# An attention's score products cut into quarters of TensorE's array

## The chip, the cores and the metric

The kernel runs on one core of a Trainium2 chip. The metric is the device time of one execution in microseconds (us); smaller is better. A core has five engines that run side by side: TensorE (PE in the profile, its weight loads PEld), VectorE (DVE), ScalarE (ACT), GpSimd (POOL) and SyncE (SP, which here only issues DMAs).

## The reference

Two parts follow each other. The first is a causal attention with decay, over 4 batches, 8 heads, 768 positions and a head width of 64; q, k and v are float32:

```
Dmask = where(i >= j, lam[h] ** (i - j), 0)
intra = (qb @ kb.T * Dmask) @ vb            # inside a block of positions
inter = (qb * lam ** (pos + 1)) @ kv_state  # from the blocks before
out   = intra + inter
kv_state = lam ** block * kv_state + (kb * lam ** (block - 1 - pos)).T @ vb
```

The second is a mixer on x, the attention's output as 4 x 768 x 512:

```
u = x + (relu(x.T @ w_tok1) @ w_tok2).T
y = u + relu(u @ w_ch1) @ w_ch2
```

## The kernel before, in words

The kernel takes blocks of 128 positions where the reference takes 64, which is the same sum: 6 blocks for each head. Heads go in pairs: 4 pairs in each of 4 batches make NI = 16 rounds of a loop (line 671). For a pair, kT and qT (made by the transposes of L230, L245 and L238) hold the 64 rows of the head width on 128 partitions: the lower 64 partitions belong to one half of the blocks, the upper 64 to the other half (x = 0 and 1), and along a row stand 6 blocks of 128 positions, three (m) for each head (h).

The function `scores` (line 313) is what the change touches. For each head h, each m and each half x it forms one block of scores, keys by queries: the weights are 64 rows by 128 columns of kT, the moving operand is 64 rows by 128 columns of qT, and the product fills 128 partitions by 128 columns of a PSUM bank sc[x]. That is 12 products for a pair of heads. The two halves x lie on different rows of the array and write different banks. All operands are float32, and the profile shows such a product as two passes, each with a weight load and a matmul, both under one line.

TensorE's order is the program's order; nothing reorders the code. One round i of the loop puts on TensorE, in this order:

- `scores(i + 1)` (L320), 24 passes in the profile;
- `carry(i)` (L348): the contribution of the earlier blocks' state, 10 products of 64x64 weights (tiles sv and st) by 128 columns, each on one quarter of the array (64 rows by 64 columns), 20 passes;
- `outputs(i, 0)` (L361): 6 products of 128x64 weights by 128 columns, 12 passes;
- `state(i + 1)` (L281): 10 products of 128x64 weights (tile kd) by 64 columns, 20 passes on the two column halves of the array;
- `outputs(i, 1)` (L361), 12 passes;
- transposes for round i + 2 (L230, in the first eight pairs L245 too), transposes of the attention's result (L386), and from round 4 on groups of the mixer's first part, `token_hidden` and `token_out` (L499, L520).

In round i = -1 there is no carry and no outputs, and `scores(0)` is followed by `state(0)`; in round 15 there are no scores. So 16 calls of `scores` run, 15 of them straight ahead of a `carry`.

Around them: VectorE multiplies the scores by the mask (`weigh`, L332, four products of 128x384 for a pair); GpSimd makes the scaled queries (L268) and places the states (L302); ScalarE copies results out of PSUM (L233, L368). SyncE issues the loads of q, k and v some rounds ahead. Where an instruction has to wait for more than it can hold itself, a semaphore instruction stands ahead of it in the same program order (EVENT_SEMAPHORE on PEldq in the profile: TensorE's sequencer, which feeds weight loads and matmuls in one stream).

The attention and its transposes end at about 172 us; the rest of the span is the channel part of the mixer (L858, L1059, L1114), with weights that are brought and split while TensorE works.

Of the kernel before, what the change touches and what calls it, by code (L numbers as in the profile page):

```python
# [25 lines left out]
def kernel(  # L26
# [23 lines left out]
    nc = tc.nc  # L50
    B, H, S, D = q.shape
# [3 lines left out]
    P = 128  # L55
# [55 lines left out]
    def bank(tag, nm, n):  # L111
        nonlocal shared
        if tag == "sh":
            tag = f"sh{shared % 3}"
            shared += 1
        return ps.tile([P, n], F32, tag=tag, bufs=4 if tag == "sc" else 1, name=nm)
# [84 lines left out]
    def rows_of(x):  # L201
        return slice(x * D, (x + 1) * D)
# [6 lines left out]
    while n < P:  # L209
        nc.vector.tensor_mul(  # L210
            out=lams[:, :, n : 2 * n], in0=lams[:, :, 0:n], in1=lams[:, :, n - 1 : n].broadcast_to([P, 2 * NP, n])
# [3 lines left out]
    for h in range(2):  # L215
        r = rows_of(h)
# [5 lines left out]
    kTs, qTs, qss, kds, weights_of, scored = {}, {}, {}, {}, {}, {}  # L222
# [90 lines left out]
    def scores(i):  # L313
        for h in range(2):
            scored[i, h] = sc = [bank("sc", f"sc{i}{x}{h}", 3 * P) for x in range(2)]
            for m in range(3):
                ms = slice((3 * h + m) * P, (3 * h + m + 1) * P)
                for x in range(2):
                    r = rows_of(x)
                    nc.tensor.matmul(  # L320
                        out=sc[x][:, m * P : (m + 1) * P],
                        lhsT=kTs[i][r, ms],
                        rhs=qTs[i][r, ms],
                        start=True,
                        stop=True,
                    )

    def weigh(i, h):
        b, p = pairs[i]
# [341 lines left out]
    for i in range(-2, NI):  # L671
# [5 lines left out]
        if 0 <= i + 1 < NI:  # L677
            scores(i + 1)
            scale_q(i + 1)
            weigh(i + 1, 0)  # L680
# [47 lines left out]
        if i in loads:  # L728
            x = loads.index(i)
# [11 lines left out]
        if i in turns:  # L741
            x = turns.index(i)
# [600 lines left out]
    for n in range(NQD):  # L1343
        r, g = divmod(n, NG)
        for s in range(7):
# [69 lines left out]
            else:  # L1415
                if n == NG and s == 0:
                    tasks.extend(lambda q_=q_: mm2(NG - 1, 1 - q_ // 4, q_ % 4) for q_ in range(8))
                if n == NG and s == 1:
                    for i in range(4):
                        x = tp.tile([P, 2, CB], F32R, tag="tt", bufs=4, name=f"tt{i}")  # L1420
                        tiles.extend((x[:, 0], x[:, 1]))
                if n == NG + 1 and s == 1:
                    for i in range(3):
                        for t in ("hh0", "hl0", "hh1", "hl1"):
                            at = dict(tag=t, name=f"{t}x{i}")
# [4 lines left out]
                    for t in ("c2h", "c2l"):  # L1430
                        x = w2b.tile([P, JG, DM], F32R, tag=t, name=f"{t}x")
# [31 lines left out]
        if n == NG - 1:  # L1463
# [8 lines left out]
            for t in ("c2h", "c2l"):  # L1472
                x = wa.tile([P, JG, DM], F32R, tag=t, name=f"{t}x")
# [45 lines left out]
```

## Time and profile before

| what | value |
|---|---|
| time, median of 3 runs | 554.69 us (554.27 to 555.03) |
| span of the profiled execution, first to last instruction | 552.4 us |
| time of the profiled execution around its span | not given; the median stands 2.29 us above the span |
| TensorE matmuls | 537.1 us busy, 97% of the span, 3710 |
| TensorE weight loads | 455.1 us busy, 82%, 3710 |
| VectorE | 386.8 us busy, 70%, 588 |
| GpSimd | 275.9 us busy, 50%, 264 |
| ScalarE | 250.2 us busy, 45%, 463 |
| DMA | 108.12 MB, mean 196 GB/s |

The span counts from the first to the last instruction on the core. Busy time is the time in which at least one instruction of the engine was running. Matmuls overlap, so the time of one group of matmuls is better read from where the groups start than from the length of one. A shape such as 64*128 64x128 means weights of 64 rows and 128 columns and a moving operand of 64 rows and 128 columns. In the timeline, consecutive instructions of one kind are merged to one row: start, time to the end of the last one, engine, line, operation, tiles, shapes, count.

### The profile page before, as it was taken

The numbers are of one execution on the slowest core, as the hardware profiler recorded it, in microseconds if no ns is written. First come the engines' busy times: TensorE is split into PE (matmuls) and PEld (weight loads), VectorE is DVE, ScalarE is ACT, GpSimd is POOL, SyncE is SP. The second block draws the span as 40 slices with busy tenths as digits, with TensorE's granted clock in tenths as the row PEclk, the third lists the DMA queues.
The fourth block names the chain that finished last, engine by engine and source line by source line (L and its number), as shares of the span: only waits on it lengthen the run. The fifth ranks groups of instructions, "written<-read, shape, count | busy, mean of one in ns | idle before, by whom it ended". The sixth has DMA issues, their size and how long they took to land.

```text
span 552.4 us, 9745 instructions
## 1 busy us (share of the span) xinstructions
PE 537.1 (97%) x3710; PEld 455.1 (82%) x3710; DVE 386.8 (70%) x588; ACT 250.2 (45%) x463; POOL 275.9 (50%) x264
## 2 busy tenths in 40 slices
PE   6999999999999999999999999999998999999996
PEld 5888989999999988788888888888886888888885
DVE  4667776677865868688995657498578864474464
ACT  3477544654534456455554344344464343233111
POOL 5555636552442777556769635545878123141000
PEclk9999999999999999999999999999999999999999
DMA  9999878698500497956777899677346987554007
GB/s 188 245 264 220 189 143 222 143 201 199 133 1 6 172 296 253 361 190 250 285 284 268 179 239 304 206 246 273 133 125 211 205 197 294 225 169 156 0 2 151
DMA packets 162942, 108.12 MB, mean 196 GB/s; under 512 B 132560, under 2 KB 147408, under 8 KB 162896
## 3 DMA queue, kind: packets, MB, share of 16 engines
q1 hardware_dynamic: 153168, 86.92, 58.4%
q10 hardware_dynamic: 9728, 20.58, 10.0%
q8 instruction: 29, 0.48, 0.4%
q14 instruction: 17, 0.14, 0.1%
HBM read 75.50 MB, written 31.98 MB: 195 GB/s over the span
## 4 chain that ended last, share of the span: by engine, by line
PE 81%; DVE 6%; ACT 5%; DMA 4%; POOL 2%; issue 2%; SPq 1%; DVEq 0%; ACTq 0%
PE b L858 15%; PE gb L1114 9%; PE po L1059 9%; PE d L858 7%; PE gc L1114 7%; PE ph L499 6%; PE pu L520 5%; PE sc L320 4%; PE xT L361 4%; PE a L858 4%; DMA raw<-in_moe_w_ch_dram 3%; PE xT L348 2%; PE gb L1059 2%; PE gc L1059 2%; PE kv L281 2%
## 5 line engine op out<-in xcount | busy, mean ns | idle before, releaser
L302 POOL COPY st<-sv 64x192 f32<-64x192 f32 (+1 forms) x32 | 15.7, 492 | 58.8 <-DVE sv L289 57.9
L1072 DVE TENSOR_TENSOR uT<-po,uT 128x512 f32<-128x512 f32 x48 | 32.8, 684 | 10.2 <-PE po L1059 9.6
L1059 PE MATMUL po<-hh,c2l 128*128 128x512 f32 x96 | 37.8, 394 | 0.0
L1059 PE MATMUL po<-hl,c2h 128*128 128x512 f32 x96 | 37.7, 392 | 0.0
L1059 PE MATMUL po<-hh,c2h 128*128 128x512 f32 x96 | 37.6, 392 | 0.0
L368 ACT COPY uT<-xT 128x384 f32<-128x384 f32 x32 | 15.2, 479 | 47.2 <-PE xT L361 47.2
L332 DVE TENSOR_TENSOR a<-sc,mask 128x384 f32<-128x384 f32 x64 | 32.1, 543 | 2.4 <-PE sc L320 2.3
L268 POOL TENSOR_TENSOR qs<-qT,lamp 128x384 f32<-128x384 f32 x32 | 32.6, 1040 | 0.0
L879 POOL TENSOR_TENSOR hl1x<-t,hh1x 128x512 fp32r<-128x512 f32 x8 | 10.6, 1326 | 41.8 <-ACT hh1x L873 41.8
L1129 DVE TENSOR_TENSOR uT<-gb,uT 128x512 f32<-128x512 f32 x40 | 26.1, 683 | 3.8 <-PE gb L1114 3.8
L393 DVE TENSOR_TENSOR xlo<-xp,xhi 128x384 fp32r<-128x384 f32 x32 | 17.7, 552 | 15.7 <-ACT xhi L392 15.2
L499 PE MATMUL ph<-xhi,w1h 128*128 128x256 f32 x96 | 28.3, 295 | 0.3 <-DVE hl L504 0.3
L499 PE MATMUL ph<-xhi,w1l 128*128 128x256 f32 x96 | 27.2, 283 | 0.0
L499 PE MATMUL ph<-xlo,w1h 128*128 128x256 f32 x96 | 27.1, 283 | 0.0
L361 PE MATMUL xT<-a,vn 128*64 128x128 f32 x384 | 27.1, 277 | 0.0
L320 PE MATMUL sc<-qT,kT 64*128 64x128 f32 x384 | 27.1, 290 | 0.0
L320 PEld LDWEIGHTS sc<-qT,kT 64*128 64x128 f32 x384 | 23.9, 197 | 3.0 <-issue 1.2
L858 PE MATMUL b<-o,c1h 128*128 128x512 f32 x72 | 25.2, 391 | 0.0
L858 PE MATMUL a<-o,c1h 128*128 128x512 f32 x72 | 25.2, 391 | 0.0
L879 POOL TENSOR_TENSOR tt<-t,tt 128x512 fp32r<-128x512 f32 x12 | 17.0, 1420 | 14.6 <-ACT tt L873 14.6
L520 PE MATMUL pu<-w2h,hh 128*128 128x384 f32 x64 | 23.2, 363 | 0.9 <-DVE uT L525 0.5
L289 DVE TENSOR_TENSOR_SCAN sv<-keep,kv 128x320 f32<-128x320 f32 x16 | 13.1, 816 | 13.3 <-PE kv L281 6.6
(417 smaller groups left out, 1737.6 us busy)
## 6 DMA issues: line engine op xcount, KB each, us to landing
c1h<-k SPq DMA_DIRECT2D x12, 896.0 KB, 5.5
c1l<-k SPq DMA_DIRECT2D x12, 896.0 KB, 7.6
raw<-in_moe_w_ch_dram SPq DMA_DIRECT2D x7, 1024.0 KB, 5.7
vn<-in_v_dram SPq DMA_DIRECT2D x16, 384.0 KB, 6.1
k<-c1h ACTq DMA_DIRECT2D x6, 896.0 KB, 5.2
k<-c1l ACTq DMA_DIRECT2D x6, 896.0 KB, 4.1
out_dram<-y SPq DMA_DIRECT2D x72, 64.0 KB, 2.5
c2lx<-k SPq DMA_DIRECT2D x7, 512.0 KB, 4.2
```

The costliest lines, as they stand in the source:

```text
L268: nc.gpsimd.tensor_mul(out=qss[i][:, h], in0=qTs[i].rearrange("p (h m i) -> p h m i", h=2, i=P)[:, h], in1=lamp[:, p, h, None, :].broadcas ...
L320: nc.tensor.matmul(out=sc[x][:, m * P : (m + 1) * P], lhsT=kTs[i][r, ms], rhs=qTs[i][r, ms], start=True, stop=True,)
L332: nc.vector.tensor_mul(out=a, in0=scored[i, h][x].rearrange("p (c i) -> p c i", i=P), in1=mask[:, 2 * p + h, None, :].broadcast_to([P, 3, P]),
L361: nc.tensor.matmul(out=xT[h * D : (h + 1) * D, m * P : (m + 1) * P], lhsT=vns[i][:, h, c, :], rhs=weights_of[i, x, h][:, m, :], start=Fals ...
L499: nc.tensor.matmul(out=ph, lhsT=w[:, c, fs], rhs=x[:, c], start=(i == 0), stop=(i == 3 * NC - 1))
L520: nc.tensor.matmul(out=pu, lhsT=h[:, kk, cs], rhs=w[:, kk, ss], start=(i == 0), stop=(i == 3 * NK - 1))
L858: nc.tensor.matmul(out=c[into], lhsT=w[:, WI[o], ct], rhs=x[:, ct], start=(first and i == 0), stop=(i == 5), skip_group_check=True,)
L879: nc.gpsimd.tensor_sub(out=B_[key][1], in0=src, in1=B_[key][0].bitcast(F32))
L1059: nc.tensor.matmul(out=po, lhsT=w[:, jj, cs], rhs=h, start=(i == 0), stop=(i == 3 * JG - 1), skip_group_check=n >= NG)
L1072: nc.vector.tensor_add(out=ub, in0=two(po), in1=ub)
L1114: nc.tensor.matmul(out=G[into, t], lhsT=w2[:, v, j, t * P : (t + 1) * P], rhs=x, start=(o in (5, 1, 2) and not second and i == 0), stop=(i ...
L1129: nc.vector.tensor_add(out=ub, in0=two(G[into, t]), in1=ub)
```

## The change

`scores` alone is changed. Each product of 64x128 weights by 128 columns is cut into four: two halves y of the weights' columns (keys) by two halves z of the moving columns (queries). Each small product has 64x64 weights and 64 moving columns, and writes 64 partitions by 64 columns of the same bank: the half y decides the partitions, z the columns. The half x still decides the rows of the array, so that (x, y) names one of four quarters. The order is z outermost, then y, then x. For a pair of heads 48 products stand in the place of 12. What is computed, the banks, the other engines' instructions, the DMAs and the order of everything else are the same.

```diff
             for m in range(3):
-                ms = slice((3 * h + m) * P, (3 * h + m + 1) * P)
-                for x in range(2):
-                    r = rows_of(x)
-                    nc.tensor.matmul(
-                        out=sc[x][:, m * P : (m + 1) * P],
-                        lhsT=kTs[i][r, ms],
-                        rhs=qTs[i][r, ms],
-                        start=True,
-                        stop=True,
-                    )
+                at = (3 * h + m) * P
+                for z in range(2):
+                    for y in range(2):
+                        for x in range(2):
+                            r = rows_of(x)
+                            nc.tensor.matmul(
+                                out=sc[x][rows_of(y), m * P + z * D : m * P + (z + 1) * D],
+                                lhsT=kTs[i][r, at + y * D : at + (y + 1) * D],
+                                rhs=qTs[i][r, at + z * D : at + (z + 1) * D],
+                                start=True,
+                                stop=True,
+                            )
```

## Rows read from the trace of the kernel before

**Rows 1.** The page: busy times, strips of 40 slices, the chain's shares by engine.

```profile
PE 537.1 (97%) x3710; PEld 455.1 (82%) x3710; DVE 386.8 (70%) x588; ACT 250.2 (45%) x463; POOL 275.9 (50%) x264
...
PE   6999999999999999999999999999998999999996
...
PEclk9999999999999999999999999999999999999999
...
PE 81%; DVE 6%; ACT 5%; DMA 4%; POOL 2%; issue 2%; SPq 1%; DVEq 0%; ACTq 0%
```

**Rows 2.** Waits of TensorE, 0 to 175 us: total, times, longest.

```profile
PE kt L230 <- DMA kn<-in_k_dram: 4.3, 1, 4.3
PE qt L245 <- ACT kT L233: 1.8, 6, 0.4
PE pu L520 <- DVE uT L525: 0.5, 1, 0.5
```

**Rows 3.** Chain of waits in order of time, one round: start, us, what, count.

```profile
123.50 1.05 PE pu L520 x6
124.56 1.54 PE sc L320 x24
126.09 0.91 PE xT L348 x19
127.00 0.81 PE xT L361 x12
127.81 0.58 PE kv L281 x20
```

**Rows 4.** Timeline of TensorE's matmuls in the same round.

```profile
124.48 1.61 PE L320 MATMUL sc<-qT,kT 64*128 64x128 f32 x24
126.02 0.38 PE L348 MATMUL xT<-qs,sv 64*64 64x128 f32 x1
126.03 0.33 PE L348 MATMUL xT<-qs,st 64*64 64x128 f32 x2
126.04 0.38 PE L348 MATMUL xT<-qs,sv 64*64 64x128 f32 x1
126.19 0.28 PE L348 MATMUL xT<-qs,st 64*64 64x128 f32 x2
126.24 0.30 PE L348 MATMUL xT<-qs,sv 64*64 64x128 f32 x2
126.30 0.28 PE L348 MATMUL xT<-qs,st 64*64 64x128 f32 x2
...
126.72 0.28 PE L348 MATMUL xT<-qs,sv 64*64 64x128 f32 x1
126.93 0.88 PE L361 MATMUL xT<-a,vn 128*64 128x128 f32 x12
127.63 0.75 PE L281 MATMUL kv<-vn,kd 128*64 128x64 f32 x20
128.21 0.83 PE L361 MATMUL xT<-a,vn 128*64 128x128 f32 x12
```

**Rows 5.** Line 320 in the whole span: duration ns min/median/max, first and last start.

```profile
L320 PEld LDWEIGHTS sc<-qT,kT x384: 182/188/336, 7.8 to 157.5; 64*128 64x128 f32 x192
L320 PE MATMUL sc<-qT,kT x384: 271/272/577, 7.8 to 157.6; 64*128 64x128 f32 x192
```

**Rows 6.** Lines 281 and 230, 36.9 to 38.9 us: the sequencer's semaphore instructions.

```profile
L281 PEldq EVENT_SEMAPHORE  x1: 1272/1272/1272, 37.0 to 37.0; - x1
...
L230 PEldq EVENT_SEMAPHORE  x1: 51/51/51, 38.8 to 38.8; - x1
```

**Rows 7.** Timeline of weight loads, 37.3 to 38.9 us.

```profile
37.57 0.64 PEld L361 LDWEIGHTS xT<-a,vn 128*64 128x64 f32 x12
38.26 0.69 PEld L281 LDWEIGHTS kv<-vn,kd 128*64 128x64 f32 x20
```

**Rows 8.** The page's DMA queues: packets, MB, share of 16 engines.

```profile
q8 instruction: 29, 0.48, 0.4%
```

**Rows 9.** Chain of waits, 185 to 245 us.

```profile
191.05 1.06 PE pu L520 x6
...
192.12 7.91 DMA raw<-in_moe_w_ch_dram
...
232.19 0.62 DVE e L898
```

## The prediction

> **What bounds the kernel now.** I read the page first, then TensorE's waits, the chain of waits, and the timeline of one round. TensorE is busy for 97% of the span, its strip shows nines almost everywhere, and 81% of the chain that ended last is its own [rows 1]. Its waits up to 175 us, the stretch in which all scores lie, come to some 7 us, of which 4.3 are the first load of k [rows 2]. So a microsecond that `scores` gains or loses on TensorE is one on the path, as long as nothing else is late behind it. In the chain the scores of one round are one piece of 1.54 us, followed at once by `carry`, `outputs` and `state` [rows 3]; 16 such pieces are 24.6 us, 4.5% of the span.
>
> [...]
>
> **The scores before, step by step.** 24 passes start between 124.48 and 124.48 + 1.61 - 0.27 = 125.82 us (0.27 is the median length of one) [rows 4, 5]. The row halves run side by side, so these are 12 rounds of two. The first pass waits for its weights: `carry`'s first on sv shows 0.38 us where a later one has 0.28, and I take the same 0.10 for the scores' first, whose weights have twice the columns [rows 4]. So 1.34 - 0.10 = 1.24 us over 11 steps, 0.112 us a round, and the stage's array time is 0.10 + 12 x 0.112 = 1.45 us. From the last start to `carry`'s first start are 126.02 - 125.82 = 0.20 us; 0.11 of it is the last round, the other 0.09 is the array running empty between two kinds of tiles. (`carry` to `outputs` has such a gap too, 126.72 to 126.93; `outputs` to `state`, both on 128x64 tiles, has none [rows 4].) Then `carry`'s first pass spends 0.10 on weights.
>
> **The scores after.** Each product is cut in four, so 96 passes of 64x64 weights by 64 columns take the place of 24. The trace shows no such pass; two rows bracket it. `state` has 64 moving columns and 64 weight columns on two column halves: 20 passes from 127.63 to 128.21, 10 rounds of 0.058 us [rows 4]. `carry` shows four quarters at work at once: four first passes start within 0.02 us, and from there each quarter starts one pass about every 0.11 us (the st pairs at 126.19 and 126.30) with twice the columns of the new pass [rows 4]. Each row of the array would be fed by the new stage just as `state` feeds it, two halves of 64 columns at a time. So I take `state`'s 0.058 us for a round of four: 96 / 4 = 24 rounds, 1.39 us, plus 0.05 for the first weights (half the columns, half the 0.10). The sum is 1.44 us against 1.45: four times the passes gain nothing in the stage itself. If a round cost half of `carry`'s 0.11 for half the columns, 0.055, it would be 0.07 us less a stage, 1.1 us in all; and if a round of four pays more than `state`'s, up to the price of `carry`'s rounds, 0.11, it is 24 x 0.11 = 2.64 us, 1.2 us more. I take 0.058, since it is nearest in columns, weights and traffic a row.
>
> The gain is behind the stage. Scores and `carry` are now the same kind of tile, 64x64. The 0.09 of running empty goes, and `carry`'s first weights load under the scores' last round (0.058 of the 0.10 hidden). That is 0.09 + 0.06 = 0.15 us for each of the 15 calls that are followed by `carry`; `scores(0)` is followed by `state`, on other tiles, and keeps its gap. Ahead of the scores stand 128x128 products as before, so that gap stays.
>
> **Can the sequencer feed it?** One round of 0.058 us takes four weight loads and four matmuls, 0.0145 us for a pair. No stretch of the trace sustains that: `state` runs at 0.029 a pass and `carry` at 0.70 / 20 = 0.035. But both are paced by the array. The sequencer alone shows at 37.0: it is held for 1.27 us ahead of `state`, the first weights load at 38.26, and at 38.8 it is already at the transposes' semaphore, having handed over 20 passes of `state` and 12 of `outputs` meanwhile [rows 6, 7]: 0.54 us for 32 pairs, 0.017 a pair at most (0.49 to 0.59 by the rounding of 38.8). At 0.017 a round is 0.068 and the stage 1.68, unless TensorE's queue is full when the stage begins; in the gap ahead of a stage it has time to fill. Its depth can be seen at 37.0 us: the sequencer is done with all 12 passes of `outputs`, whose first weights load at 37.57, while the last of `carry` are still to run [rows 6, 7], so some 16 pairs wait. 80 x 0.017 = 1.36 is under the 1.39 of the rounds. I take no loss, and 0.24 a stage as the dear end.
>
> Added beside this: 72 passes x 2 x 16 = 2304 instructions. The 7420 that stand there came in 29 packets of code [rows 1, 8], 256 each, so nine more come, each taking 0.4% x 16 x 552.4 / 29 = 1.2 us on the queues. TensorE has no wait that answers to the 29; I cost the nine at nothing, and at 9 x 1.2 = 10.8 us if none is hidden. VectorE gets the first head's scores when half the rounds are over, as before; DMAs and other engines' work do not change.
>
> **The sum.** 15 x 0.15 = 2.25 us off, 16 x 0.01 off for the stage itself, which I leave out. What is late next: behind the attention the chain leaves TensorE once, from a load of raw weights at 192.12 to VectorE at 232.8, where TensorE waits about 0.6 us; but that load follows TensorE's pu at 191.05 to 192.11, so it comes earlier along with it [rows 9]. The span goes from 552.4 to 550.2, and the 2.3 us by which the median stands above the span stay: 552.5.
>
> [...] Side by side, first starts on different quarters stand 0.01 us apart [rows 4]. [...]
>
> **The rivals.**
> - *One pass at a time, or two quarters at a time* (slower). If starts of passes are paced by what the trace has sustained at best, `state`'s 0.029, or if a product's second pass holds back the next quarter so that only two quarters ever work, a stage is 96 x 0.029 = 2.78 us: 1.33 more, less 0.15: 15 x 1.18 + 1.33 = 19 us, 573.7. It decides from the point where a pass costs over (1.45 + 0.15) / 96 = 0.0167 us. For it: nothing below 0.028 is sustained anywhere. Against: the four quarters of `carry`, and the 0.017 of the sequencer.
> - *Rounds a little dearer* (no change). At the sequencer's 0.068 a round the stage is 1.68, 0.23 dearer, and 15 x 0.08 + 0.23 = 1.4 us more: 556.1; at 0.064 the stage is 1.59 and the gain is just used up: 554.7. For it: the queue's depth is only inferred, and four streams write PSUM at once. Against: `carry`'s rounds on four quarters, 0.11, are no longer than those of `outputs` on two halves (126.93 to 127.63, six rounds of 128 columns, 0.117 with the first weights) [rows 4].
> - *Code arrives late* (slower). Nine packets at 1.2 us, less 2.25: 563.2 with none hidden, 557 with half. For it: the new instructions lie within 150 us, in bursts. Against: 29 packets without a visible wait.
>
> **Chances.** Forecast 0.58, its own range 551.4 (rounds of 0.055) to 553.6 (half the gain lost); rounds a little dearer 0.17, half of it within 0.2%, a quarter on either side; one or two at a time 0.15; late code 0.10. The measurement can tell about 0.2%, 1.1 us, from no change. Faster by more: 0.58 + 0.04 = 0.62. Within: 0.08 + 0.04 from late code that costs about what is gained: 0.12. Slower: 0.26. The range reaches from 551.3 up to 561, which leaves out the one-at-a-time rival and the dear half of late code.
>
> **What would show it.** Right: L320 x1536, a stage from first score to first `carry` of about 1.45 us, `carry` starting some 0.06 after the last score pass, without the 0.20; four score passes within 0.06. Wrong: a score stage of over 1.6 us in the chain; passes 0.025 or more apart throughout; new idle time named issue ahead of L320 or L348 where code packets land; or TensorE idle behind 192 us by what was gained ahead of it.

## The result, and the profile after

The kernel with 48 products a pair of heads takes 557.68 us (median, 556.18 to 559.54) against 554.86 us before: ratio 1.0057, 95% interval 1.0041 to 1.0073. It is 2.8 us slower where 2.2 us less was forecast (554.69 to 552.5). The profiled execution took 556.63 us, with a span of 554.8 us against 552.4.

The page after (busy times, instructions; strips; the queue that brings code):

```profile
span 554.8 us, 12049 instructions
...
PE 537.3 (97%) x4862; PEld 456.2 (82%) x4862; DVE 385.8 (70%) x588; ACT 250.3 (45%) x463; POOL 276.8 (50%) x264
...
PE   6899999999999999999999999999999999999996
...
PEclk9989999999999999999999999999999999999999
...
q8 instruction: 38, 0.62, 0.5%
```

Against [rows 1, 8]: 1152 passes more on TensorE and the same busy time; nine more packets of code; and one slice of the clock strip, the third, that was a 9 and is an 8.

The timeline of TensorE's matmuls in the round that answers to [rows 4] (start, us to the end of the last, count at the end):

```profile
127.03 1.63 PE L322 MATMUL sc<-qT,kT 64*64 64x64 f32 x96
128.48 0.32 PE L350 MATMUL xT<-qs,sv 64*64 64x128 f32 x1
128.48 0.28 PE L350 MATMUL xT<-qs,st 64*64 64x128 f32 x2
128.50 0.33 PE L350 MATMUL xT<-qs,sv 64*64 64x128 f32 x1
...
129.13 0.28 PE L350 MATMUL xT<-qs,sv 64*64 64x128 f32 x1
129.33 0.43 PE L363 MATMUL xT<-a,vn 128*64 128x128 f32 x3
```

The part of the prediction that was worked out came as forecast. From the first score to the last are 1.63 - 0.22 = 1.41 us (0.22 is one pass), 0.07 more than the 1.34 of before; `carry` starts 0.04 us behind the last score, where it was 0.20; and from the first score to `outputs` are 129.33 - 127.03 = 2.30 us against 126.93 - 124.48 = 2.45. That is 0.15 us gained, to the hundredth the forecast for a round; the rounds differ by 0.02 around 0.14.

The loss lies elsewhere. TensorE's waits up to 175 us, in the order of [rows 2] (total, times, longest):

```profile
PE kt L230 <- DMA kn<-in_k_dram: 4.7, 1, 4.7
PE xT L363 <- issue: 2.2, 3, 1.9
PE qt L245 <- ACT kT L233: 1.4, 5, 0.3
```

The middle row is new: `outputs` waits for nothing that the profile shows. The chain of waits from 22 us on, and the row of before that answers to its last one:

```profile
22.42 0.74 PE xT L350 x19
23.16 0.81 PE xT L363 x12
23.97 0.58 PE kv L281 x20
24.55 0.44 PE xT L363 x8
24.99 1.89 issue
26.88 0.44 PE xT L363 x4
27.32 1.32 PE kt L230 x6
28.64 1.47 PE qt L245 x6
30.11 1.09 PE xp L388 x6
31.20 1.56 PE sc L322 x96
```

```profile
28.10 1.54 PE sc L320 x24
```

In the middle of `outputs`, after 8 of its 12 passes, TensorE stands still for 1.89 us. The passes behind the standstill read no tile that the passes ahead of it had not read already, so there was no new operand to wait for. What follows is slow: six transposes of k take 1.32 us here and 0.81 in later rounds of the same kernel. The scores that began at 28.10 us begin at 31.20. The stretches of this time (us; busy and count of PE, PEld, DVE, ACT and POOL; granted clock; DMA share; GB/s) say why the transposes are slow:

```profile
24.70:26.90 2.20, 0.31 (x8) 0.17 (x5) 2.20 (x5) 0.00 (x0) 0.93 (x2) 1.00 1.19 255
26.90:28.50 1.60, 1.60 (x11) 1.43 (x11) 0.30 (x1) 0.89 (x2) 0.72 (x1) 0.67 0.96 273
28.50:31.20 2.70, 2.70 (x17) 2.20 (x18) 0.00 (x0) 2.08 (x6) 1.27 (x2) 0.56 1.23 228
31.20:33.00 1.80, 1.80 (x112) 1.80 (x114) 0.30 (x1) 1.80 (x4) 0.69 (x1) 1.00 0.88 276
```

Behind the standstill the granted clock is 0.67 and then 0.56 of full (0.50 from 27.60 to 30.90 us), until the scores of the next pair, where it is 1.00 again. The transposes of k, of q and of the result take 1.32 + 1.47 + 1.09 = 3.88 us; in later rounds, at a granted clock of 1.00, they take 0.81, 1.09 (twice 0.55 for three) and 0.66: 2.56. So the standstill costs 1.3 us more after it has ended.

**What TensorE waited for is its own code.** Counted in the order of their starts, weight loads, matmuls and semaphore instructions together, 962 instructions of TensorE's queue had started when it stood still. Up to 175 us it stood still four more times with no wait to explain it, for 0.3 to 0.4 us each, and always a multiple of 256 instructions from that count:

| instructions started | standstill ended at | last packet of code landed at | between |
|---|---|---|---|
| 962 = 194 + 3 x 256 | 26.88 us | 25.30 us | 1.58 us |
| 1474 = 194 + 5 x 256 | 39.14 | 37.74 | 1.41 |
| 1986 = 194 + 7 x 256 | 49.17 | 47.68 | 1.49 |
| 5314 = 194 + 20 x 256 | 139.41 | 138.20 | 1.22 |
| 5826 = 194 + 22 x 256 | 152.23 | 150.85 | 1.38 |

One packet of q8 is 16 KB (0.62 MB in 38 packets), and I count 256 instructions to it: the five counts lie 512, 512, 3328 and 512 apart, all multiples of 256, and 7514 instructions in 29 packets before and 9818 in 38 after are 259 and 258 to a packet. The number of packets is that of the bounds 194 + 256k that a program crosses: 29 for 7514 instructions before, 38 for 9818 after. In the trace after, up to 175 us, 22 of 25 packets began to move 0.5 to 4.0 us after TensorE had crossed a bound (the other three 0.25 to 1.3 us ahead of it), each moved for 0.9 to 1.4 us, and where TensorE waited for one, it went on 1.2 to 1.6 us after that. No trace shows what calls for a packet; my assumption is that it is called for at one bound and needed at the next: from the bound before to the end of the standstill are 5.6, 6.4, 3.4, 4.2 and 4.1 us in the five rows. Before, the first bounds are crossed at 15.2, 23.3, 31.3 and 39.2 us, 8 us apart, and from the second on the packet has landed over 4 us ahead. After, they are crossed at 10.4, 14.9, 21.2 and (without the standstill) about 24.8 us: 256 instructions in 3.6 us, and the packet is not there. A short block alone does not make a standstill: the one from 82.2 to 85.2 us lasted 3.0 us and passed without one, since its packet had landed at 83.13.

The kernel before crosses 29 bounds, and the waits of its matmuls show no idle time named issue over the whole span. Here TensorE stood still at five of 38 bounds, for 1.89 us at one of them.

The sum: 15 x 0.14 = 2.1 us gained; 3.4 us lost at the five bounds (starts 2.16 us apart where 0.11 is usual, and 0.28, 0.35, 0.40 and 0.33 over the usual); 1.3 us lost to the clock. That makes 2.6 us slower; TensorE's last transpose of the attention starts 2.83 us later than before (172.04 against 169.21 us), and the span is 2.4 us longer. The 1.3 us of the clock belong to this profiled execution: another of the four had a mean granted clock of 1.000 and took 558.73 us, and what it paid instead is open.

### The profile page after: what moved, and what is told of

It is laid out like the page before. It is cut to its first block, busy times and chain, and to the rows that moved or that the text cites. A ratio compares the mean times of both kernels' runs of the same rounds, so it can differ in the third digit from the quotient of the medians.

```text
span 554.8 us, 12049 instructions
## 1 busy us (share of the span) xinstructions
PE 537.3 (97%) x4862; PEld 456.2 (82%) x4862; DVE 385.8 (70%) x588; ACT 250.3 (45%) x463; POOL 276.8 (50%) x264
## 4 chain that ended last, share of the span: by engine, by line
PE 78%; DVE 6%; ACT 5%; DMA 4%; issue 2%; SPq 2%; POOL 2%; DVEq 0%; ACTq 0%
PE b L860 15%; PE gb L1116 9%; PE po L1061 8%; PE d L860 7%; PE gc L1116 7%; PE ph L501 5%; PE pu L522 4%; PE a L860 4%; PE xT L363 4%; PE sc L322 3%; DMA raw<-in_moe_w_ch_dram 3%; PE gb L1061 2%; PE xT L350 2%; PE gc L1061 2%; DMA qn<-in_q_dram 1%
## 5 line engine op out<-in xcount | busy, mean ns | idle before, releaser
L1074 DVE TENSOR_TENSOR uT<-po,uT 128x512 f32<-128x512 f32 x48 | 32.8, 684 | 10.4 <-PE po L1061 9.8
L370 ACT COPY uT<-xT 128x384 f32<-128x384 f32 x32 | 15.2, 480 | 49.3 <-PE xT L363 49.3
L395 DVE TENSOR_TENSOR xlo<-xp,xhi 128x384 fp32r<-128x384 f32 x32 | 17.7, 552 | 18.3 <-ACT xhi L394 17.9
L322 PEld LDWEIGHTS sc<-qT,kT 64*64 64x64 f32 x1536 | 25.0, 139 | 3.5 <-issue 1.3
L322 PE MATMUL sc<-qT,kT 64*64 64x64 f32 x1536 | 27.3, 225 | 0.3 <-ACT qT L246 0.2
L363 PEld LDWEIGHTS xT<-a,vn 128*64 128x64 f32 x384 | 20.6, 137 | 4.4 <-issue 2.4
```

The lines of the kernel that those rows point to most:

```text
L322: nc.tensor.matmul(out=sc[x][rows_of(y), m * P + z * D : m * P + (z + 1) * D], lhsT=kTs[i][r, at + y * D : at + (y + 1) * D], rhs=qTs[i][r ...
L363: nc.tensor.matmul(out=xT[h * D : (h + 1) * D, m * P : (m + 1) * P], lhsT=vns[i][:, h, c, :], rhs=weights_of[i, x, h][:, m, :], start=Fals ...
L1074: nc.vector.tensor_add(out=ub, in0=two(po), in1=ub)
```

## The experiments

Three theories were put against each other: the code theory above; that work on four quarters costs the time itself; that TensorE, being early, meets some wait at that place. The kernel before, run beside the first four, took 554.59 us.

**The same quarters with half the passes.** The columns of the weights are cut (y), the moving columns are not (z):

```diff
-                for z in range(2):
-                    for y in range(2):
-                        for x in range(2):
+                for y in range(2):
+                    for x in range(2):
...
-                                out=sc[x][rows_of(y), m * P + z * D : m * P + (z + 1) * D],
+                            out=sc[x][rows_of(y), m * P : (m + 1) * P],
...
-                                rhs=qTs[i][r, at + z * D : at + (z + 1) * D],
+                            rhs=qTs[i][r, at : at + P],
```

> Scores as 24 products of 64x64 weights by 128 columns, on the same quarters: 48 passes a pair of heads instead of 96 (before: 24). Code theory (TensorE's instructions come in blocks of 256, a block is asked for when the one before is entered, and the changed kernel runs through a block faster than the next one comes): the 0.14 us a round gained between scores and carry stays, as carry is still the same kind of tile, and 768 more instructions than before instead of 2304 leave at most one short stall: 552.3 to 553.5 us, ratio to before 0.996 to 0.998, no idle time named issue over 0.5 us ahead of outputs. Quarters theory (work on four quarters at once costs the time itself): the quarters are as busy as in the changed kernel, so it is slower than before as that one is, 556 to 558. Wait theory (TensorE, being early, meets a semaphore or data wait at the second outputs of round 1): as early as the changed kernel, so the same stall of about 2 us there, 556 to 558.

Measured: 553.12 us, ratio 0.9973, interval 0.9962 to 0.9983. It is faster than both. Its chain of waits in the round of [rows 3]:

```profile
124.65 1.47 PE sc L321 x48
126.12 0.68 PE xT L349 x19
126.80 0.81 PE xT L362 x12
```

Scores and `carry` together take 2.15 us here, 2.45 before, and 1.56 + 0.75 = 2.31 with 48 products. The quarters are used as much as in the slow kernel, at half the instructions, and 32 packets of code come without one standstill by issue of 0.3 us or more in its waits up to 175 us. That rules the quarters theory out, and the wait theory too, since TensorE is earlier still at that place (24.21 us against 24.38 at the start of the second `outputs` of round 1). But 15 x 0.30 = 4.5 us were to be had in this way and 1.5 arrived. Two places keep the rest in the profiled execution. In the first rounds the chain is a load:

```profile
19.15 15.12 DMA qn<-in_q_dram x2
34.27 0.14 issue
34.41 0.30 PE qt L245
```

TensorE waits 2.1 us for q there (two waits), and the seventh call of `scores` starts 1.15 us later than before (55.91 against 54.77 us). The two loads landed at 26.70 and 34.27 us; in the kernel before they landed at 25.32 and 31.84 us, 0.7 and 1.4 us ahead of the transposes that use them, so a gain on TensorE larger than these margins would have met the loads there too, unless they came earlier with it. The DMA strip of the kernel before shows nines in these slices of 13.8 us:

```profile
DMA  9999878698500497956777899677346987554007
```

Why the loads landed later here, no run tells. From the seventh call to the sixteenth it gains 1.86 us in nine rounds, 0.2 each. And where the attention's last transpose is 0.98 us earlier than before, the matmuls behind 230 us are only 0.50 us earlier: in between lie the raw weights' load and conversion of [rows 9]; that these hold it back was not tested.

**Quarters in the late rounds only, and in the early ones only.**

```diff
+                if i < 5:        # the other kernel: if i >= 5
+                    ms = slice((3 * h + m) * P, (3 * h + m + 1) * P)
+                    for x in range(2):
+                        ...      # the 12 old products
+                    continue
```

> The 48 small products only for pairs 5 to 15, the 12 old ones for pairs 0 to 4. Code theory: the long stall of 1.9 us lies in round 1 and is gone, with the slow clock behind it; 11 rounds gain 0.14 each, 1.5 us, and up to three stalls of 0.3 us are given back: 553.3 to 554.4, ratio 0.997 to 0.999. Quarters theory: 11 of 16 parts of the loss of 2.8 us: 556.8. Wait theory: about as the code theory.

> The 48 small products only for pairs 0 to 4, the 12 old ones from pair 5 on. Code theory: the stall of about 2 us in round 1 and the slow clock behind it (1.3 us) are still there, four gains of 0.14 us: 557 to 558, as slow as the changed kernel or slower. Quarters theory: 5 of 16 parts of 2.8 us: 555.7. Wait theory: 557 to 558 too.

Measured: late only 554.29 us, ratio 0.9997 (0.9985 to 1.0009); early only 557.14 us, ratio 1.0040 (1.0028 to 1.0052). Five calls in the early rounds lose nearly as much as all sixteen, and eleven in the late ones lose nothing. The early one's timeline of TensorE has the standstill again, 2.67 us long, after the same 962 instructions and the same 8 passes:

```profile
24.33 0.61 PE L375 MATMUL xT<-a,vn 128*64 128x128 f32 x8
27.61 0.44 PE L375 MATMUL xT<-a,vn 128*64 128x128 f32 x4 [2.67 <-issue]
```

Here the clock did not fall, though the standstill is the longest of all; the stretch behind it reads:

```profile
27.60:29.00 1.40, 1.39 (x13) 1.16 (x12) 0.00 (x0) 0.86 (x3) 0.21 (x1) 1.00 1.13 240
```

Hardly anything else in this kernel gains or loses up to the attention's end: its fourth call of `scores` starts 2.63 us later than before (30.66 against 28.03 us), its last transpose of the attention 2.48 us later (171.69 against 169.21). So a single late block makes up nearly the whole of its 2.55 us.

The late one shows no standstill by issue in its list of waits up to 175 us, and its late rounds gain what they should: its seventh call starts 0.61 us later than before and its sixteenth 0.46 us earlier, 0.12 a round. Yet this does not show in the time. In the profiled execution TensorE waits 0.9 us for a load of q in the early rounds, where the scores are the old ones, and 0.8 us for a copy (snap, ACT) near 390 us. I take the first for the scatter of loads in the rounds that DMA fills, which no run shows; the second is open.

**The bounds moved.** Only the very first call has its old products, so that 144 instructions fewer stand ahead of everything else:

```diff
+                if i == 0:
+                    ...          # the 12 old products
+                    continue
```

> As the changed kernel, but the first call of scores, pair 0, has its 12 old products: 144 instructions fewer ahead of all the rest. Code theory: the bounds of the blocks of 256 fall 144 instructions later in the program. The stall ahead of the 9th pass of the second outputs in round 1 (instruction 962 by count) is gone from there; if any comes, it comes again at instruction 962, now within the scores of pair 3, and shorter, since transposes that wait for copies lie in that block: 0 to 1 us. The short stalls of later rounds move to other lines as well. Time 553 to 556. Quarters theory: within 0.3 us of the changed kernel. Wait theory: the stall stays at the second outputs of round 1, at another count (818), and the time is within 0.3 us of the changed kernel.

Measured: 558.03 us, ratio 1.0053 (1.0040 to 1.0066): no better than the changed kernel, where 553 to 556 was expected. The time alone would fit the quarters theory. The place does not:

```profile
17.36 0.39 PE L375 MATMUL xT<-a,vn 128*64 128x128 f32 x4
19.71 0.55 PE L375 MATMUL xT<-a,vn 128*64 128x128 f32 x6 [1.95 <-issue]
```

The long standstill is gone from round 1 and stands a round earlier, after 450 = 194 + 256 instructions; its packet landed at 18.19 us, 1.5 us ahead of the end. Two more, of 0.31 and 0.72 us, stand at 1474 and 2754, again bounds (194 + 5 x 256, 194 + 10 x 256). So the standstills go by the count, which the wait theory excludes. My expectation erred in looking at the one bound that I knew: a shift lays every bound on another stretch, and the dense stretch of the round before got one. Behind this standstill the clock is low as well: granted 0.68 from 19.7 to 22.3 us and 0.50 from there to 24.0.

**The other half of the cut.** Moving columns cut, weights whole, on the two row halves of before:

```diff
-                ms = slice((3 * h + m) * P, (3 * h + m + 1) * P)
-                for x in range(2):
+                at = (3 * h + m) * P
+                for z in range(2):
+                    for x in range(2):
...
+                            lhsT=kTs[i][r, at : at + P],
+                            rhs=qTs[i][r, at + z * D : at + (z + 1) * D],
```

> The other half of the cut alone: 64x128 weights, 64 moving columns, two row halves, 24 products and 48 passes a pair of heads. As many instructions as the kernel with 64x64 weights by 128 columns, so the code theory sees no stall. The loads of 128 weight columns were 0.107 us apart on a half before, and a pass of 64 columns streams in about 0.055, so the loads set the pace: 24 rounds of 0.107 instead of 12 of 0.112, 1.2 us more a stage, and the gap to carry stays 0.2: 16 x 1.2 = 19 us slower, 573 to 575. If weight loads were hidden or halved with the columns, it would be as before, 554.6.

Measured: 577.79 us against 554.61 beside it, ratio 1.0423 (1.0380 to 1.0465), somewhat above what was expected. The timeline of its scores, and line 321 from 100 to 180 us (min/median/max ns):

```profile
140.57 2.90 PE L321 MATMUL sc<-qT,kT 64*128 64x64 f32 x48
143.40 0.38 PE L349 MATMUL xT<-qs,sv 64*64 64x128 f32 x1
```

```profile
L321 PEld LDWEIGHTS sc<-qT,kT x336: 182/188/188, 103.4 to 178.7; 64*128 64x128 f32 x168
```

48 passes on two halves are 24 rounds, and from first to last start 2.90 - 0.27 = 2.63 us: 0.11 a round, as with 128 moving columns [rows 4]. Halving the moving columns alone shortened nothing; with the weights' columns halved too, on four quarters, a round took 0.06 (24 in 1.41 us). That fits the expectation that the loads of 128 weight columns set the pace. The stage grew by 1.29 us, 16 times 20.6, and the profiled execution (575.33 us) is 20.7 above the median of the kernel before; two of the four runs lie near 580 us, and what those paid is open.

**Code alone, by no-ops.** The old scores, with empty instructions behind each product:

```diff
                         stop=True,
                     )
+                    for _ in range(12):   # the other kernel: 4
+                        nc.tensor.nop("pad")
```

> The kernel before, its 12 products of 64x128 by 128 kept, with 12 empty instructions (no-ops) on TensorE's queue behind each product: 2304 more instructions, as many as the change adds, and no more array work. Code theory: the array's work is as before, but the blocks of 256 are used up as fast as in the changed kernel, so idle time named issue of 1 us or more appears in the first rounds, at counts 256 apart with the no-ops included, and the time is 556 to 560 us. Quarters theory (the quarters cost it): no quarters here, 554.6, unless the no-ops themselves hold up the sequencer, which would show as idle time within the scores of every round. Wait theory (TensorE too early at one place): TensorE is not early, 554.6.

> As the run with 12 no-ops, but with 4 behind each product: 768 more instructions, as many as the kernel with 24 products of 64x64 by 128 adds. Code theory: as that kernel, which showed no stall by code, none here either; no gain between scores and carry, so 554.3 to 555.2, the same as before. If no-ops were dear by themselves, a third of the loss of the run with 12.

Measured: 713.79 us and 572.28 us, ratios 1.2871 (1.2854 to 1.2889) and 1.0326 (1.0301 to 1.0352). Both missed, and neither bears on the question, since the no-ops slow TensorE down, so that a block of 256 instructions lasts about as long as before or longer. 159.2 us over 2304 no-ops are 69 ns each, with a granted clock of 0.70 from 20 to 60 us and 0.72 from 60 to 120 us included; 17.7 us over 768 are 23 ns each. The waits and the timeline of the run with 12 show the sequencer late inside the scores of every round:

```profile
PE sc L320 <- issue: 29.3, 83, 0.6
```

```profile
60.94 0.46 PE L320 MATMUL sc<-qT,kT 64*128 64x128 f32 x2 [0.50 <-issue]
61.85 0.46 PE L320 MATMUL sc<-qT,kT 64*128 64x128 f32 x2 [0.46 <-issue]
```

A no-op is no cheap stand-in for a weight load or a matmul, which went through the sequencer at 8.5 ns or less [rows 6, 7]. No run adds code and nothing else. The code theory rests on the counts, on the shift of the bounds, and on the pair above: 96 passes and 48 passes on the same quarters, 557.68 and 553.12 us.

## Why the prediction was wrong

- *TensorE bounds the attention, and a microsecond there is one on the path*: true of a loss, since the 2.5 us of the early-only kernel are still there at the attention's end. A gain arrives behind 55 us; in the first rounds the kernel with 24 products, faster on TensorE, waits for q.
- *The stage costs 1.44 us against 1.45*: first start to `carry`'s first 1.45 against 1.54. The rounds of four quarters took 0.059 us (1.41 us less 0.05 for the first weights, over 23 steps) where 0.058 was taken.
- *Scores and carry on the same tile save 0.15 us a round*: 0.14 to 0.15, shown. `carry` starts 0.16 us closer behind the last score and takes 0.06 less to `outputs` (0.85 against 0.91), and the stage is 0.07 longer.
- *The sequencer can feed it*: shown. 96 pairs in 1.41 us are 0.0147 us each, without idle time inside the stage except at a bound.
- *"I cost the nine at nothing"*: this step failed. It took the 29 packets before, which no wait answered to, as proof that code is always in time, and priced only the nine that come in addition. It looked for late code ahead of the scores and `carry`; the longest standstill came inside `outputs`. What decided here was not how many packets there are but how soon 256 instructions are used up: `scores`, `carry`, `outputs` and `state`, 148 passes, make 296 instructions in 3.7 us (1.56 + 0.74 + 0.81 + 0.58 in the chain) where 76 passes made 152 in 3.84 [rows 3]. Any packet in that stretch could be late, old or new. In the profiled execution five were, and cost 3.4 us.
- The rival of late code was there, at 0.10, with 557 us for packets that are half hidden (5.4 us less 2.25 make 557.8 by its own terms). That the time came out at it is luck: its sum was half of nine packets, the trace's is five standstills, at old and new packets alike, and the clock, which it did not have. The clock added 1.3 us: a standstill of 2 us cost over 3 us where it fell behind it. The measured time also lies within the stated range of 551.3 to 561, on the side of that rival and not of the forecast.
- *What is late next behind 192 us* was taken to move along. The kernel with 24 products shows that some of it does not: 0.98 us earlier became 0.50.

What remains open is why a packet starts to move up to 4 us after the bound in the first rounds and as little as 0.5 us later on. The DMA engines are mostly busy when it is late: from the bound before to the landing of the five late packets their busy share by the profile was 1.29, 1.16, 1.21, 1.10 and 0.66. No run took their load away.

## What to carry to other kernels

When products are cut smaller, count instructions against time: for each stretch, how long 256 instructions of one engine last, and hold that against the time from one bound to the use of the packet that I assume it calls for, 3.4 to 6.4 us at the standstills of the changed kernel. Cut the side that buys something, here the weights' columns, which put the scores on the tiles of the next stage; halving the moving columns as well doubled the instructions for nothing here. And a stage's own arithmetic can be right to 0.01 us while the time is decided by a queue that the stage never names.

## What the runs showed of the hardware

- Two stages on the same kind of tile followed each other without a gap in the changed kernel: 0.04 us from the last score's start to `carry`'s first, within one round of 0.06, against 0.20 between 64x128 and 64x64 tiles with rounds of 0.11 in the kernel before.
- Rounds of 128 moving columns were the shorter way on the quarters: 12 of them took 1.54 - 0.27 = 1.27 us from first to last start, 24 of 64 columns took 1.41.
- After two of the three long standstills the granted clock of TensorE was low, though the engine was working again: 0.67 from 26.9 to 28.5 us and 0.56 from there to 31.2 in the changed kernel, 0.68 from 19.7 to 22.3 us and 0.50 from there to 24.0 with the bounds moved. After the third and longest, 2.67 us, with quarters in the early rounds only, it was 1.00, as it was after those of 0.3 to 0.4 us in the changed kernel. So the length of these standstills alone does not say whether the clock fell.
- A no-op on TensorE's queue cost up to 69 ns in rows of twelve (159.2 us over 2304) and 23 ns in rows of four (17.7 us over 768).
- Code came in packets of 16 KB, as many as there are bounds 256 instructions apart: 29 before, 38 after. Where TensorE stood still at a bound in the changed kernel, it went on 1.2 to 1.6 us after the packet had landed; where the packet had landed 2.1 us or more ahead of the bound, no standstill of 0.3 us or more stood there (up to 175 us). In the kernel before, up to 175 us, each had landed over 4 us ahead.
